# A deadline queue for weight loads, and transposed tiles made in other places

## The chip, the cores and the metric

The kernel runs on one core of one Trainium2 chip. The metric is the device time of one execution in microseconds (us); lower is better. A kernel's time is the median of its runs. The profile's span is about 1.8 us shorter than the time of the same execution (1098.9 us against 1100.72 us for the kernel before), and all times inside a profile count from the start of that span.

## The reference

`x` is 2048 tokens of 1024 values, in bf16. A normalised `x` goes through attention with 32 heads of 32 values, and through a second normalisation and an MLP with 3584 hidden values. The two are multiplied and added to `x`. Cut to what matters:

```python
def _A_ref(x, wqkv, wo):                       # attention, H = 32, Dh = 32
    qkv = (x @ wqkv).reshape(B, S, 3, H, Dh).transpose(2, 0, 3, 1, 4)
    q, k, v = qkv[0], qkv[1], qkv[2]
    p = _softmax(einsum("bhqd,bhkd->bhqk", q, k) * (Dh ** -0.5), axis=-1)
    o = einsum("bhqk,bhkd->bhqd", p, v)
    return o.transpose(0, 2, 1, 3).reshape(B, S, D) @ wo

def _B_ref(x, w1, b1, w2, b2):                 # MLP, F = 3584
    y = _layernorm(x, axis=-1)
    h = _gelu(einsum("bsd,df->bsf", y, w1) + b1)
    return einsum("bsf,fd->bsd", h, w2) + b2

xn = _layernorm(x, axis=-1)
return x + _A_ref(xn, wqkv, wo) * _silu(_B_ref(xn, w1, b1, w2, b2))
```

## The kernel before

The kernel is a host program that writes one instruction list per engine. It walks through 512 units. Each unit has eight score matmuls on PE, two exponentials of 128x1024 on ACT, one filler item on PE (a piece of the MLP, or of the next heads' q, k and v), and the matmuls of the weighted sum (PV). Units 0 to 7 are the prologue: unit p also projects K and Q of the p-th pair of 128-token tiles, then V. For that it needs `xnT`, the normalised `x` with the features on the partitions, one tile after another. Tiles below `TDMA` are transposed on PE and copied by ACT; the others are transposed by DMA. All DMAs are issued by SP, in the order of its list, so a DMA on SP's list waits for everything ahead of it there.

```python
TDMA = 4
def transp(tb):
    i = tb % NXN
    if tb >= TDMA:
        op("sync", lambda e: e.dma_start_transpose(xnT[:, :, tb * 128:(tb + 1) * 128], xnb[i]),
           r=[("xnb", i)], w=[("xnT", tb)], dma=f"xt{tb % 4}", c=256)
        return
    ...                                        # else 8 PE transposes and one ACT copy

def pro_unit(p):                               # units 0 to 7
    if p + 3 < NP:
        norm_pair(p + 3)                       # statistics and normalisation on VectorE; issues transp()
    if p == 3:
        load_bias()
    if p >= 2:
        ynorm_pro(p - 2)                       # the second normalisation of tile p-2, on ACT
    if 4 <= p:
        load_sub(0, p - 4)                     # the first w1 piece (war), a quarter a unit
    pair_kq(p)                                 # 16 matmuls 128x128 by 256
    for t in range(2 * p + 2, 2 * p + 4):
        if t < TDMA:
            transp(t)
    pair_v(p)                                  # 16 more
    ...
def ynorm_pro(tb):
    if tb < 3:
        xt = xst[:, tb * D:(tb + 1) * D]
        op("scalar", lambda e: e.activation(xt, xt, ACT.Identity, ...), ...)
        op("sync", lambda e: e.dma_start(y_d[tb * 128:(tb + 1) * 128, :], xt), ...)   # to a scratch tensor
```

The MLP runs over chunks of 352 tokens. Its input `yTc` (the second normalisation `y`, transposed) is read back from the scratch tensor `y_d` by DMA transposes, at unit 5 for the first chunk. Its weights pass through two buffers (`war`), and the 256 KB pieces of a buffer are put one into each of the following units. The loads of the output stage (`wo`, the residual `xres`, the gate `gres` as a transpose) are spread by unit number as well:

```python
if u == 5:
    for s4 in range(4):
        load_y(0, s4)
...
for v in sorted(k for k in sp_tasks if k <= u):        # sp_tasks[unit] = loads
    for fn, *a in sp_tasks.pop(v):
        fn(*a)
...
if state["qi"] == q_end:                               # the last q, k, v item is done
    tail["xfree"] = pg.lists["tensor"][-1]
    for h in range(HG):
        sp_tasks[u + 1 + 2 * h].append((load_wo, h))
    for t in range(NTB):
        sp_tasks[u + 2 + 4 * t].append((load_xres, t))
...
def pre():                                             # first part of an output item
    if k == 0:
        if tb == 0:
            for t in range(NTB):
                load_gres(t)
```

The host program has a clock model, with a cost for every instruction, only to decide the order in which it writes work into the lists.

The softmax here doesn't subtract the row's maximum and nothing guards it: scores larger than these inputs give would overflow.

## Time and profile before

| | before |
|---|---|
| time, median of 3 runs (lowest to highest) | 1101.85 us (1101.66 to 1102.9) |
| span of the profile | 1098.9 us |
| PE busy, ACT busy | 98%, 95% |
| first scores (unit 0) start at | 17.11 us |
| unit 0 to unit 20 | 61.02 us |
| unit 20 to unit 448 | 876.33 us |
| unit 448 to unit 480 | 64.18 us |
| the rest | 80.26 us |

A stage is read from the timeline as the distance between the first score matmuls of two units.

The page gives the busy time of each engine (part 1: us, share of the span, instructions) and the chain of work that ended last (part 4), for the kernel before:

```profile
PE 1074.6 (98%) x29089; PEld 700.4 (64%) x29089; DVE 629.1 (57%) x1413; ACT 1041.3 (95%) x1190; POOL 20.0 (2%) x63
...
PE 57%; ACT 40%; DVE 1%; DMA 1%; issue 0%; SPq 0%; POOL 0%
```

PE and ACT are both nearly full, and the chain alternates between them. Only what holds up one of these two can cost time. The timeline of PE in the kernel before shows where that is a DMA (columns: start in us, duration in us, engine, line, operation, output and input tiles, shapes, count, and in brackets the idle time before it with its releaser):

```profile
23.52 1.92 PE L675 MATMUL ps<-xnT,wq 128*128 128x256 bf16 x16 [1.53 <-DMA xnT<-hT]
...
46.03 1.92 PE L675 MATMUL ps<-xnT,wq 128*128 128x256 bf16 x16
47.79 1.91 PE L691 MATMUL ps<-wq,xnT 128*128 128x256 bf16 x16
...
54.04 1.11 PE L398 MATMUL ps<-yTc,war 128*32 128x352 bf16 x16 [0.71 <-DMA war<-in_B_w_dram]
...
57.07 0.40 PE L398 MATMUL ps<-wq,xnT 128*32 128x256 bf16 x8 [0.29 <-DMA wq<-in_A_wqkv_dram]
```

The third pair's K and Q projection (23.52) waited 1.53 us for tiles 4 and 5. The first MLP weights came 0.71 us late (54.04). SP's own timeline in the kernel before, where the duration is the time SP takes to issue, shows why:

```profile
18.73 15.05 SPq L382 DMA_TRANSPOSE xnT<-hT  x8
33.83 0.57 SPq L754 DMA_DIRECT2D y_scratch<-OT  x1
35.27 2.60 SPq L382 DMA_TRANSPOSE xnT<-hT  x2
...
38.88 0.37 SPq L754 DMA_DIRECT2D y_scratch<-OT  x1
39.36 2.64 SPq L382 DMA_TRANSPOSE xnT<-hT  x2
...
45.04 5.17 SPq L514 DMA_TRANSPOSE yTc<-y_scratch  x4
50.25 1.09 SPq L493 DMA_DIRECT2D war<-in_B_w_dram  x2
```

A DMA transpose costs SP 1.3 us of issue (2.60 us for two). The four transposes of `y` hold SP from 45.0 to 50.2 us, and the weights that PE wants at 53 us stand behind them.

### The profile page before, as it was taken

How to read it: one execution, taken by the hardware profiler on the slowest of the kernel's cores; microseconds unless marked ns; L12 is line 12 of the kernel's file. 1: busy time of each engine (PE TensorE's matmuls, PEld its weight loads, DVE VectorE, ACT ScalarE, POOL GpSimd, SP SyncE). 2: the span in 40 equal slices, each digit the busy share in tenths (PEclk: the TensorE clock that was granted, in tenths of full speed). 3: DMA queues.
4: the chain of work that ended last, by engine and by line, in shares of the span. 5: the costliest groups of instructions: out<-in, count | busy, mean ns of one | idle time of the engine just before them, and what ended most of it. 6: DMA issues, size and time to landing. Idle time of an engine off the chain costs nothing.

```text
span 1098.9 us, 61692 instructions
## 1 busy us (share of the span) xinstructions
PE 1074.6 (98%) x29089; PEld 700.4 (64%) x29089; DVE 629.1 (57%) x1413; ACT 1041.3 (95%) x1190; POOL 20.0 (2%) x63
## 2 busy tenths in 40 slices
PE   6999999999999999999999999999999999999998
PEld 4766666666666666666666666666666666666665
DVE  8488753377742477652276852277743378624566
ACT  4799999899999999999999999999999999999994
POOL 2400000000000000000000000000000000000000
PEclk9999999999999999999999999999999999999999
DMA  8764256323373224333432334433244324386453
GB/s 249 182 204 138 77 111 175 112 80 109 95 159 96 90 80 128 99 73 105 131 121 80 118 72 133 141 112 109 80 86 136 100 93 147 112 252 115 96 143 99
DMA packets 211624, 132.97 MB, mean 121 GB/s; under 512 B 54698, under 2 KB 202154, under 8 KB 211370
## 3 DMA queue, kind: packets, MB, share of 16 engines
q1 hardware_dynamic: 211370, 129.02, 43.1%
q8 instruction: 228, 3.74, 1.4%
q14 instruction: 26, 0.21, 0.1%
HBM read 104.87 MB, written 12.58 MB: 107 GB/s over the span
## 4 chain that ended last, share of the span: by engine, by line
PE 57%; ACT 40%; DVE 1%; DMA 1%; issue 0%; SPq 0%; POOL 0%
ACT P L836 36%; PE ps L398 34%; PE ps L824 9%; PE ps L853 6%; PE ps L856 6%; ACT u L558 3%; PE ps L675 1%; PE ps L691 1%; DVE stats L326 1%; DMA OT<-in_A_x_dram 1%; ACT thz L601 0%; DMA wq<-in_A_wqkv_dram 0%; DMA xnT<-hT 0%; DVE hT L359 0%; SPq L286 0%
## 5 line engine op out<-in xcount | busy, mean ns | idle before, releaser
L836 ACT ACTIVATE P<-ps 128x1024 bf16<-128x1024 f32 x1024 | 969.7, 1075 | 16.5 <-PE ps L824 10.5
L853 PE MATMUL ps<-P,VP 128*32 128x256 bf16 x4096 | 256.6, 273 | 0.0
L856 PE MATMUL ps<-P,ones 128*32 128x256 bf16 x4096 | 256.5, 273 | 0.0
L398 PE MATMUL ps<-yTc,war 128*32 128x352 bf16 (+1 forms) x5376 | 226.2, 309 | 1.9 <-issue 1.1
L398 PE MATMUL ps<-hT,war 128*32 128x352 bf16 (+1 forms) x5376 | 225.3, 309 | 0.0
L824 PE MATMUL ps<-QT,KT 32*128 32x256 bf16 x4096 | 203.7, 273 | 8.1 <-ACT P L836 5.0
L398 PEld LDWEIGHTS ps<-yTc,war 128*32 128x32 bf16 x5376 | 127.6, 96 | 76.8 <-DVE xb L541 17.3
L398 PEld LDWEIGHTS ps<-hT,war 128*32 128x32 bf16 x5376 | 128.0, 96 | 73.9 <-issue 25.5
L597 DVE TENSOR_SCALAR zh<-ps,b2h 128x352 f32<-128x352 f32 (+1 forms) x48 | 27.5, 573 | 204.4 <-PE ps L398 204.4
L824 PEld LDWEIGHTS ps<-QT,KT 32*128 32x128 bf16 x4096 | 61.0, 92 | 120.6 <-issue 64.2
L541 DVE TENSOR_SCALAR xb<-ps,b1T 128x352 f32<-128x352 f32 (+1 forms) x168 | 96.1, 572 | 63.7 <-PE ps L398 60.0
L853 PEld LDWEIGHTS ps<-P,VP 128*32 128x32 bf16 x4096 | 109.6, 97 | 21.1 <-issue 1.5
L856 PEld LDWEIGHTS ps<-P,ones 128*32 128x32 bf16 x4096 | 109.6, 97 | 18.4
L564 DVE SCALAR_TENSOR_TENSOR hT<-u,xb 128x352 bf16<-128x352 f32 (+1 forms) x168 | 83.8, 508 | 61.3 <-ACT u L558 61.2
L398 PE MATMUL ps<-xnT,wq 128*32 128x352 bf16 (+1 forms) x2688 | 112.7, 309 | 0.0
L398 PEld LDWEIGHTS ps<-xnT,wq 128*32 128x32 bf16 x2688 | 64.0, 96 | 36.8 <-DVE xb L541 10.2
L551 DVE SCALAR_TENSOR_TENSOR u<-u,xb 128x352 f32<-128x352 f32 (+1 forms) x168 | 82.6, 508 | 1.9
L547 DVE TENSOR_TENSOR u<-xb 128x352 f32<-128x352 f32 (+1 forms) x168 | 82.6, 508 | 0.9
L558 ACT ACTIVATE u<-u 128x704 f32<-128x704 f32 (+1 forms) x84 | 70.6, 840 | 0.0
L398 PE MATMUL ps<-xnT,OT 128*32 128x352 bf16 (+1 forms) x1536 | 62.9, 309 | 0.2 <-DVE wq L658 0.2
L398 PE MATMUL ps<-wq,xnT 128*32 128x256 bf16 x1536 | 51.0, 274 | 0.3 <-DMA wq<-in_A_wqkv_dram 0.3
L398 PEld LDWEIGHTS ps<-xnT,OT 128*32 128x32 bf16 x1536 | 37.5, 97 | 19.9 <-DVE wq L658 8.1
(50 smaller groups left out, 468.1 us busy)
## 6 DMA issues: line engine op xcount, KB each, us to landing
war<-in_B_w_dram SPq DMA_DIRECT2D x336, 256.0 KB, 4.1
wq<-in_A_wqkv_dram SPq DMA_DIRECT2D x36, 128.0 KB, 4.2
OT<-in_A_x_dram SPq DMA_DIRECT2D x16, 256.0 KB, 5.6
y_scratch<-OT SPq DMA_DIRECT2D x16, 256.0 KB, 2.5
xnT<-in_A_x_dram SPq DMA_DIRECT2D x16, 256.0 KB, 4.3
out_dram<-wq SPq DMA_DIRECT2D x16, 256.0 KB, 2.0
gT_scratch<-gst SPq DMA_DIRECT2D x40, 88.0 KB, 1.7
xnT<-in_A_wo_dram SPq DMA_DIRECT2D x8, 256.0 KB, 3.6
```

The costliest lines, as they stand in the source:

```text
L326: op("vector", lambda e, c=c: e.bn_stats(stats[:, tb, c, :], xt[:, c * 512:(c + 1) * 512]), r=[("xst", tb)], w=[("st", tb, c)], c=677.0)
L398: ins = e.matmul(outs(j), lhsT=lhs(j), rhs=rhs, start=start, stop=stop, tile_position=(0, 32 * j), skip_group_check=True)
L541: x0 = op("vector", lambda e: e.tensor_scalar(xb[:, 0:n], bank(bk, 0, n), b1T[:, f:f + 1], None, op0=ALU.add), r=[("b", bk), "b1"], w=[kx] ...
L547: x = op("vector", lambda e: e.tensor_tensor(ub[:, 0:n], xb[:, 0:n], xb[:, 0:n], op=ALU.mult), r=[kx], w=[ku], c=151 + 1.042 * n)
L551: x = op("vector", lambda e: e.scalar_tensor_tensor(ub[:, 0:n], ub[:, 0:n], 1.0 / 0.044715, xb[:, 0:n], op0=ALU.add, op1=ALU.mult), r=[kx, ...
L558: x = op("scalar", lambda e: e.activation(ut[:, :, 0:n], ut[:, :, 0:n], ACT.Tanh, scale=0.7978845608028654 * 0.044715), r=kus, w=kus, c=48 ...
L564: op("vector", lambda e: e.scalar_tensor_tensor(hT[:, fq, 0:n], ut[:, i, 0:n], 1.0, xq[:, 0:n], op0=ALU.add, op1=ALU.mult), r=[kus[i], kq] ...
L597: x0 = op("vector", lambda e: e.tensor_scalar(zh[:, 0:n], bank(bk, 0, n), 0.25, b2h[:, nb:nb + 1], op0=ALU.mult, op1=ALU.add), r=[("b", bk ...
L824: ins = e.matmul(bank(bks[j], kh * 256, (kh + 1) * 256), lhsT=KT[i2][32 * j:32 * j + 32, k0:k0 + 128], rhs=QT[i2][32 * j:32 * j + 32, qb * ...
L836: op("scalar", lambda e, p=p, sl=sl: e.activation(pb[:, 2 * p:2 * p + 2, :, :].rearrange("p a b q -> p (a b q)"), ps[:, sl * 1024:(sl + 1) ...
L853: e.matmul(bankq(ACC, j, 0, QW), lhsT=VP[vp][:, kb, vo + 32 * j:vo + 32 * j + 32], rhs=pb[:, j, kh, :], start=first, stop=False, tile_posi ...
L856: ins = e.matmul(bankq(ACC, j, QW, 2 * QW), lhsT=ones[:, 0:32], rhs=pb[:, j, kh, :], start=False, stop=last, tile_position=(0, 32 * j), sk ...
```

## The change

The change wants to take the remaining DMA waits away from PE, and to make the loads follow their deadlines. It has five parts.

1. Tiles 4 and 5 are transposed on PE too (`TDMA` 6).
2. The first chunk's three `y` tiles go by DMA transpose from SBUF straight into `yTc`, and their normalisation moves one unit earlier. They are no longer read back from the scratch tensor (the third, of which the next chunk needs a part, is still stored there as well).
3. The first four weight pieces are loaded at units 2 to 5 in place of 4 to 7.
4. A queue sorted by deadline replaces `sp_tasks`. One load is taken per unit, two if more than three are due, each held until the last PE instruction so far is done (`pace`); in an even unit a normalisation may take their place. A load that is needed and still queued is issued on demand. The output stage's loads are in the queue, the first four `gres` transposes too.
5. The clock model's constants change.

The diff, cut to its core:

```diff
-        TDMA = 4
+        TDMA = 6
@@ prologue
-            if p >= 2:
-                ynorm_pro(p - 2)
-            if 4 <= p:
-                load_sub(0, p - 4)
+            if p >= 1:
+                ynorm_pro(p - 1)
+            if 2 <= p < 2 + 4:
+                load_sub(0, p - 2)
@@ ynorm_pro
-                op("sync", lambda e: e.dma_start(y_d[tb * 128:(tb + 1) * 128, :], xt), ...)
+                m = min(128, CW - tb * 128)
+                op("sync", lambda e: e.dma_start_transpose(yTc[:, :, tb * 128:tb * 128 + m], xt[0:m, :]), ...)
+                if m < 128:
+                    op("sync", lambda e: e.dma_start(y_d[tb * 128:(tb + 1) * 128, :], xt), ...)
-            if u == 5:
-                for s4 in range(4):
-                    load_y(0, s4)
@@ the queue
+        def soon(prio, tag, fn, *a):
+            due.append((prio, len(due), tag, fn, a))
+            due.sort(key=lambda z: z[0])
+        def run_due(tag=None):
+            i = 0 if tag is None else next((i for i, z in enumerate(due) if z[2] == tag), None)
+            ...
+            fn(*a)
-                for v in sorted(k for k in sp_tasks if k <= u):
-                    for fn, *a in sp_tasks.pop(v):
-                        fn(*a)
+                if u % 2 == 0 and ys and not any(z[0] < cnt["piece"] + 2 for z in due):
+                    ynorm(ys.pop(0))
+                else:
+                    pace[:] = pg.lists["tensor"][-1:]
+                    for _ in range(1 + (len(due) > 3)):
+                        run_due()
+                    pace.clear()
@@ output stage
                     for h in range(HG):
-                        sp_tasks[u + 1 + 2 * h].append((load_wo, h))
+                        soon(NPC + 2 * h, ("wo", h), load_wo, h)
                     for t in range(NTB):
-                        sp_tasks[u + 2 + 4 * t].append((load_xres, t))
+                        soon(NPC + 16, ("xres", t), load_xres, t)
+                        soon(NPC + 16, ("gres", t), load_gres, t)
@@ clock model
-            self.dma_clk = max(t, self.dma_clk) + 4.4 * c
+            self.dma_clk = max(t, self.dma_clk) + 3.4 * c
-                t = max(t, self.clk[eng] + 103.0)
-                span += max(120.0 - one, 0.0)
+                t = max(t, self.clk[eng] + (98.0 if mode == "col" else 105.0))
+                span += 11.0
[... cut: wq and w1/w2 pieces put into the queue with soon(), on-demand calls of run_due() in the items ...]
```

## The prediction

> **What bounds the kernel now.** The page gives PE 98% and ACT 95% of a 1098.9 us span; the chain that ended last is PE 57%, ACT 40%, DMA 1%. From 57 us on the loop alternates between a full PE and a full ACT: a unit with a w1 item repeats every 2.07 us on PE (timeline, 57.84, 59.91, 61.98), two exponentials every 1.83 us on ACT. The windows view has PE idle for 7.3 of the 880 us from 120 to 1000 us. The waits view shows no PE wait on a DMA after 57.3 us. The long waits are SP's own (380 us before war loads) and cost nothing.
>
> **What is exposed** lies before 60 us. In timeline and waits, PE waits 7.5 us for the first normalised tile (untouched), 1.53 us at 23.5 us for the DMA transpose of tiles 4 and 5 (issued at 18.7), 0.45 us for ACT at 52.2, 0.71 us for war at 54.0, 0.29 us for wq at 57.1. On SP the four y transposes take 45.0 to 50.2 us; two war and four wq loads queue behind them.
>
> **Costs and gains.**
> 1. Tiles 4 and 5 on PE: removes the 1.53 us wait; adds 1.2 to 1.4 us of PE (16 transposes took 1.37 us at 14.06) and 1.9 us of ACT (two evictions, 1.94 us at 15.02). The first y normalisation (about 1.15 us of ACT) moves from the time of that wait into the same crowded unit. My sum puts the third pair's KQ matmuls at 24.1 us instead of 23.5: zero or a loss of up to 0.7 us. Later pairs keep their 4.48 us period, bound by PE.
> 2. y straight from SBUF: removes the scratch round trip of chunk 0 and 5.2 us of SP at 45 to 50 us. With war loaded two units earlier the 0.71 us wait goes.
> 3. wq for the second V pair starts before 51.4 us, but pacing holds its last parts until the next unit's scores, so the 0.29 us wait may stay or grow to 1 us. Net of 2 and 3: 1 to 2 us gained.
> 4. Paced loads in the loop: about one load a unit; 256 KB landed in 4.1 us (DMA issues), two units. I expect no new waits.
> 5. Altered cost constants move each unit of the host's schedule model by under 10 ns. They may reorder VectorE tasks and tanh; either sign, 2 to 3 us. Evictions already hold weight loads for some 65 us in total (waits of PEld).
> 6. Tail: gres loads go earlier, but PE never waited for them.
>
> The Trainium skill ("DMA: Bandwidth & Descriptors", "Issuing engines are not separate DMA queues") says all issuers share 16 DMA engines; that agrees with a gain from order, not bandwidth (mean DMA share 43%).
>
> **Predicted:** 1098.5 us, about 0.3% faster; range 1094 to 1102.5. Faster by over 2%: 0.02; within 2%: 0.95; slower by over 2%: 0.03.
>
> **Right or wrong.** Right: no DMA wait on xnT near 23 us, KQ of the third pair at 23.5 to 24.3 us; no y transposes at 45 to 50 us; no war wait at 54 us; the tenth unit's scores at 56 to 57.5 us instead of 57.84; the later span within 3 us of before. Wrong: PE waits on war or wq in the loop (a load popped only on demand costs about 4 us), or a third pair later than 25 us.
>
> **What would make it wrong.** The queue serving weights late at the changes between w1, w2 and wq; or new constants improving the interleaving of ACT and PE by more than I allow, where up to 10 us lie.

## The result, and the profile after

The changed kernel is correct. It ran at 1103.52 us (1102.71 to 1104.61, 4 runs) against 1102.38 us for the kernel before (1101.66 to 1102.97, 4 runs) in the same rounds: a ratio of 1.0011, with an interval of 0.9994 to 1.0029. A ratio here and below is the mean time of one kernel's fast runs over that of the other's of the same rounds, so it is not quite the ratio of the quoted medians. The change is worth nothing measurable, and the prediction of 1098.5 us (1094 to 1102.5) missed.

For scale: the 32 runs of the kernel before that were made beside the experiments lie between 1099.8 and 1105.5 us. One trace of each is therefore not enough, and both kernels were traced twice more (experiments e13 to e16). The stages in all six traces, in us:

| trace | first scores | unit 0 to 20 | of it unit 6 to 7 | of it unit 7 to 10 | 20 to 448 | 448 to 480 | span |
|---|---|---|---|---|---|---|---|
| before | 17.11 | 61.02 | 4.48 | 8.20 | 876.33 | 64.18 | 1098.9 |
| before, e13 | 17.28 | 62.51 | 4.48 | 10.24 | 876.16 | 64.28 | 1100.5 |
| before, e15 | 16.85 | 62.52 | 4.48 | 8.22 | 876.00 | 65.67 | 1101.3 |
| after | 17.70 | 63.16 | 8.22 | 6.55 | 875.53 | 65.85 | 1102.5 |
| after, e14 | 17.43 | 63.58 | 8.18 | 6.55 | 875.85 | 68.28 | 1105.4 |
| after, e16 | 17.06 | 62.32 | 6.09 | 6.95 | 875.51 | 66.42 | 1101.7 |

The rest, from unit 480 to the end, takes 80.3 to 80.4 us in every trace. Between the means of the three traces, the change costs 1.0 us up to unit 20, gains 0.5 us in the loop and costs 2.1 us from unit 448 to 480. The first traces alone give 3.6 us of longer span: 0.59 at the first scores, 2.14 up to unit 20, minus 0.80 in the loop, and 1.67 from 448 to 480. The start of the first scores (16.5 to 18.1 us over all traces) follows the moment when the PE clock comes up (13.4 to 16.6 us in the clock record) and not the change.

The same two parts of the page, for the kernel after:

```profile
PE 1077.6 (98%) x29105; PEld 701.4 (64%) x29105; DVE 630.4 (57%) x1413; ACT 1043.0 (95%) x1192; POOL 20.0 (2%) x63
...
PE 54%; ACT 44%; DVE 1%; DMA 1%; SPq 0%; issue 0%
```

PE has 16 instructions and 3.0 us more to do: the 16 transposes, and matmuls that ran slower for a while. PE's timeline in the kernel after:

```profile
21.96 1.92 PE L699 MATMUL ps<-wq,xnT 128*128 128x256 bf16 x16 [1.11 <-ACT QT L689]
...
24.70 1.92 PE L683 MATMUL ps<-xnT,wq 128*128 128x256 bf16 x16
...
49.28 3.00 PE L683 MATMUL ps<-xnT,wq 128*128 128x256 bf16 x16 [2.00 <-DMA xnT<-hT]
52.08 2.54 PE L699 MATMUL ps<-wq,xnT 128*128 128x256 bf16 x16
54.55 0.40 PE L836 MATMUL ps<-QT,KT 32*128 32x256 bf16 x8
```

The wait of 1.53 us for tiles 4 and 5 is gone. In its place PE waits 1.11 us for ACT at 21.96, and the third pair starts at 24.70 us. The waits for `war` and `wq` are gone too: unit 7 to unit 10 takes 6.55 us in place of 8.20. But the eighth pair now waits 2.00 us for its DMA transposes, and then its 16 matmuls take 3.00 and 2.54 us where they took 1.92 and 1.91. SP's timeline in the kernel after:

```profile
36.42 2.59 SPq L379 DMA_TRANSPOSE xnT<-hT  x2
39.06 0.60 SPq L310 DMA_DIRECT2D brow<-in_B_b_dram  x1
39.72 0.27 SPq L311 DMA_DIRECT2D brow<-in_B_b_dram  x1
40.03 1.22 SPq L763 DMA_TRANSPOSE yTc<-OT  x1
41.30 0.59 SPq L766 DMA_DIRECT2D y_scratch<-OT  x1
41.92 0.44 SPq L503 DMA_DIRECT2D war<-in_B_w_dram  x1
42.46 4.28 SPq L379 DMA_TRANSPOSE xnT<-hT  x2
```

Each entry starts within 0.1 us of the end of the one before: SP is the resource that is full here. The `y` transposes and the first weight loads now stand ahead of tiles 14 and 15, which are issued at 42.46 us where they were issued at 39.36 us, and take 4.28 us to issue in place of 2.64. The windows view of the kernel after (window, length, busy us and instruction count of PE, PEld, DVE, ACT and POOL, then the granted clock, the DMA share and GB/s) shows the rest:

```profile
45.00:50.00 5.00, 3.00 (x44) 2.11 (x43) 0.00 (x0) 2.78 (x5) 3.93 (x15) 0.99 0.93 210
50.00:55.00 5.00, 5.00 (x41) 3.42 (x42) 0.00 (x0) 1.00 (x3) 0.00 (x0) 0.66 0.03 9
```

After the wait the granted clock is 0.66 over the next 5 us. The clock record holds it at one half for 3413 ns and at full speed otherwise; 3.413 us at a half in 5 us make 0.66. The DMA engines are nearly idle by then (0.03), so the slow matmuls are a matter of the clock.

Late in the kernel, the timeline of PE shows holes in the middle of a unit that wait for no semaphore, as here in the kernel after:

```profile
975.49 0.28 PE L865 MATMUL ps<-P,VP 128*32 128x256 bf16 x4
975.60 0.28 PE L868 MATMUL ps<-P,ones 128*32 128x256 bf16 x4
976.63 0.29 PE L865 MATMUL ps<-P,VP 128*32 128x256 bf16 x4 [0.75 <-issue]
```

The windows view there, of the kernel before:

```profile
975.00:980.00 5.00, 4.95 (x156) 3.59 (x151) 0.97 (x2) 5.00 (x8) 0.00 (x0) 1.00 0.95 289
980.00:985.00 5.00, 5.00 (x164) 3.72 (x156) 0.98 (x2) 4.53 (x6) 0.00 (x0) 1.00 0.67 199
985.00:990.00 5.00, 5.00 (x158) 3.44 (x152) 1.19 (x3) 4.91 (x7) 0.00 (x0) 1.00 0.60 173
```

and of the kernel after:

```profile
975.00:980.00 5.00, 4.25 (x132) 2.92 (x124) 1.23 (x4) 4.58 (x6) 0.00 (x0) 1.00 0.97 290
980.00:985.00 5.00, 5.00 (x160) 3.48 (x154) 0.97 (x2) 4.71 (x7) 0.00 (x0) 1.00 1.10 249
985.00:990.00 5.00, 4.41 (x140) 2.96 (x132) 0.98 (x2) 3.84 (x5) 0.00 (x0) 1.00 0.84 245
```

PE falls from full to 4.25 and 4.41 us of 5, while the DMA share stays about 1 for ten microseconds longer. The queue has bunched the output stage's loads together with the last weight pieces: in SP's timeline five `wo` loads go out in a row at 962.00 us, where the kernel before sends them one at a time, the last at 980.02 us.

### The profile page after: what moved, and what is told of

It reads as the page before. It is cut to its first block, busy times and chain, and to the rows that moved or that the text cites. A ratio compares the mean times of both kernels' runs of the same rounds, so it can differ in the third digit from the quotient of the medians.

```text
span 1102.5 us, 61718 instructions
## 1 busy us (share of the span) xinstructions
PE 1077.6 (98%) x29105; PEld 701.4 (64%) x29105; DVE 630.4 (57%) x1413; ACT 1043.0 (95%) x1192; POOL 20.0 (2%) x63
## 3 DMA queue, kind: packets, MB, share of 16 engines
q8 instruction: 228, 3.74, 1.5%
## 4 chain that ended last, share of the span: by engine, by line
PE 54%; ACT 44%; DVE 1%; DMA 1%; SPq 0%; issue 0%
ACT P L848 39%; PE ps L395 32%; PE ps L836 9%; PE ps L865 5%; PE ps L868 5%; ACT u L565 4%; PE ps L683 1%; PE ps L699 1%; DMA xnT<-hT 0%; ACT thz L609 0%; SPq L379 0%; DMA OT<-in_A_x_dram 0%; PE ps L386 0%; DVE stats L323 0%; ACT xnT L389 0%
```

## The experiments

Two theories came out of the traces. **Theory A**: the new `y` transposes and early weight loads fill SP, so that tiles 14 and 15 are issued late, and the wait that follows also brings a stretch of half clock. **Theory E**: in the tail, the doubled rate of the queue and the early `gres` transposes fill the DMA engines, and PE then runs dry because its instructions are fetched late. Their rivals were: **B**, the bytes of the weight loads and not SP's order delay the transposes; **C**, the queue or the constants make the whole loop slower (the table above refutes it: unit 20 to 448 takes 875.5 to 875.9 us after and 876.0 to 876.3 before); **D**, the third pair's later start (part 1) delays everything after it; **F**, the pacing or the clock constants cause the loss in the tail.

In all of them "before" is the kernel before in the same rounds. All kernels gave correct results. Each run also reports its mean granted clock: 0.998 or less in every traced run with a stretch of half clock after the start, and 0.999 or 1.0 in every traced run without.

### e1: the weight loads back at units 4 to 7

```diff
-            if 2 <= p < 2 + 4:
-                load_sub(0, p - 2)
+            if 4 <= p:
+                load_sub(0, p - 4)
```

> Edit to the changed kernel: only the four war loads of the prologue go back to units 4 to 7, as before the change; the y transposes stay early. Theory A (SP order): the last two xnT transposes (tiles 14, 15) were issued at 42.46 us and landed near 49 us because SP, which spends about 1.3 us on each transpose, had y work and war loads of units 2 and 3 in front of them. Two war loads (0.57 and 0.44 us) then account for about 1 us of the 3 us delay: issue of tile 14 near 41.3 us, the wait of the eighth pair's KQ falls from 2.0 us to under 1 us, and the half-clock window after it (3.4 us, worth 1.7 us) goes[...]. Rival B (the 16 DMA engines are full, the war bytes of 0.5 MB slow the transposes): the wait goes altogether, because the war bytes were what held the transposes. Rival C (the paced queue or the constants make the loop slower): no change of the total. A: 2 to 3.5 us faster than the changed kernel's slower runs (span near 1099.5 to 1100.5).

Measured: 1102.87 us against 1103.24 us, ratio 0.9999 (0.9982 to 1.0016). The wait of the eighth pair fell from 2.00 to 0.57 us; tile 14 was issued at 41.99 us. Unit 6 to 7 took 5.12 us, with no half clock in it. The weight loads ahead of the transposes are part of the cause, and not all of it. They do not act by their place on SP alone: tile 14 was expected at 41.3 us, and measured from the first scores (which began 0.28 us earlier here) it was issued only 0.2 us sooner than in the kernel after. More came from the issue of the two transposes, which took 3.56 us in place of 4.28. The median is 0.65 us below the changed kernel's, where 2 to 3.5 us were expected.

### e2: the third `y` tile's transpose behind tiles 14 and 15

```diff
+            if p == 4:
+                yturn_pro(2)          # the DMA transpose and the store of y tile 2, no longer in ynorm_pro
```

> Edit to the changed kernel: only the transpose of y tile 2 and its store to scratch are put behind the transposes of tiles 14 and 15; war loads stay early. Theory A: takes 1.2 + 0.6 us of SP away from in front of them; tile 14 issued near 40.5 us, the wait of the eighth pair's KQ under 0.7 us, no half-clock window, span 1099 to 1100. Rival B (war bytes on full DMA engines): the wait stays near 2 us, since the early war loads stay. Rival C: no change of the total.

Measured: 1102.47 us against 1103.24 us, ratio 0.9999 (0.9982 to 1.0016). SP's timeline in e2:

```profile
39.87 0.40 SPq L503 DMA_DIRECT2D war<-in_B_w_dram  x1
40.37 2.59 SPq L379 DMA_TRANSPOSE xnT<-hT  x2
```

Tile 14 was issued at 40.37 us, PE did not wait for `xnT` at all, and unit 6 to 7 took 4.53 us. All weight loads stayed where the change had put them, so their bytes alone are not the cause: in that form rival B is refuted. What counts is what stands ahead on SP. (The `y` tile's SP time and its bytes moved together, so the run does not separate these two.) The long issue of tiles 14 and 15 also goes with the `y` tile's transpose and store directly ahead of it: it took 4.28 us in the kernel after, 3.56 in e1 and 4.31 in e4, where they stand there, and 2.59 us in e2 and e3, where they do not. The DMA share does not explain it (0.78 during the 4.28 us, and 0.78 during the 2.64 us of the kernel before); the reason stays open.

### e3: both

```diff
[the edits of e1 and e2]
```

> Edit to the changed kernel: both of the above. Theory A: tile 14 issued as soon as VectorE has normalised it (39.3 us), no wait of the eighth pair's KQ, no half-clock window; its loop starts (scores of the eighth unit) near 50.8 us instead of 54.55, scores of the eleventh unit near 57.4 us against 57.84 of the kernel before and 61.10 of the changed one; span 1098.5 to 1099, time about 0.3 to 0.5 us below the kernel before, 3.5 us below the changed kernel's slower runs. Rival C: the loop part after the eleventh unit is longer than before's 1041.1 us and the total stays at 1102 or more.

Measured: 1101.42 us against 1103.24 us, ratio 0.9992 (0.9977 to 1.0008). Timelines of e3, SP first, then PE:

```profile
39.55 2.59 SPq L379 DMA_TRANSPOSE xnT<-hT  x2
42.20 1.97 SPq L770 DMA_TRANSPOSE yTc<-OT  x1
...
46.62 1.92 PE L683 MATMUL ps<-xnT,wq 128*128 128x256 bf16 x16
...
50.22 0.40 PE L843 MATMUL ps<-QT,KT 32*128 32x256 bf16 x8
```

Tile 14 is issued at 39.55 us, nearly where the kernel before had it. The eighth pair waits for nothing, runs at full clock, and the scores of unit 7 start at 50.22 us in place of 54.55. Unit 0 to 20 takes 59.47 us, 3.7 us less than in the changed kernel's first trace and 1.6 us less than in the best trace of the kernel before. Theory A holds, and the gain that was predicted for parts 2 and 3 is there. The median shows little of it (0.3 to 0.5% was expected), because the tail still loses (unit 448 to 480: 66.37 us).

### e4: `TDMA` back to 4

```diff
-        TDMA = 6
+        TDMA = 4
```

> Edit to the changed kernel: tiles 4 and 5 go back to DMA transposes, all else kept. Theory A: the transposes of tiles 14 and 15 are late as before (SP is busy without a break from tile 8 on, and tiles 4 and 5 come well ahead of that), so the 2.0 us wait and the half-clock window stay; the third pair's KQ waits for the DMA again, about 1.5 us, and starts near 23.5 to 24 us: span within 1 us of the changed kernel's 1102.5. Rival D (transposing tiles 4 and 5 on PE is what cost): span falls to 1099 or less.

Measured: 1103.87 us against 1103.24 us, ratio 1.0016 (0.9997 to 1.0036). The third pair started at 23.60 us again, but the eighth pair waited 2.34 us and a half clock followed. PE also waited 1.27 us for the bias load (`brow`), which SP issued at 39.27 us, behind two `y` transposes and a weight load; the changed kernel shows this wait in e14 and e16 too (0.4 and 0.8 us), the kernel before in none of its traces. Rival D is refuted: the eighth pair's wait does not come from the third pair. Nor does part 1 make it shorter: measured from the first scores, tile 14 was issued after 24.55 us here and after 24.76 us in the kernel after.

### e5: e3, and the first four `gres` transposes back at the first output item

```diff
 [the edits of e3]
                 if k == 0:
+                    if tb == 0:
+                        for t in range(NTB):
+                            load_gres(t)
...
-                        soon(NPC + 16, ("gres", t), load_gres, t)
```

> Edit to the run with y tile 2 and war late: the gres transposes of the first four output tiles go out when the first output item begins, as before the change, instead of from the queue right after the last war piece. In all five traces of the changed family PE lost 1.7 to 3.5 us between units 457 and 464 (about 972 to 990 us) against the kernel before; the gaps lie in the middle of matmul groups that wait for no semaphore, each ends with an instruction fetch of 16 KB on queue 8, and the DMA share there is 1.0 to 1.2 against 0.6 to 0.95 before. Theory E (the queue bunches loads at the end: gres transposes and xres beside the last war pieces fill the 16 DMA engines, PE's instruction fetch comes late): the gaps between 975 and 990 us go, DMA share there under 1.0; a gap near 972 us may stay; the loss between units 457 and 464 falls from about 2.2 us to under 1 us; span 1097 to 1098.3. Rival F (PACE waits or the constants cause it): the loss stays at about 2.2 us.

Measured: 1100.34 us against 1102.01 us, ratio 0.9978 (0.9963 to 0.9993). Unit 448 to 480 took 65.54 us where e3 took 66.37. That is the direction of theory E, but the step is smaller than the spread of the changed kernel's own traces (65.85 to 68.28 us). The expectation was met in part: between units 457 and 464, where the loss sits, the run took 16.13 us against 14.78 in the kernel before, so 1.35 us remained where under 1 us was expected. PE still had one issue gap of 0.7 us.

### e6: e3, and the second load per unit only when weight pieces are due

```diff
 [the edits of e3]
-                    for _ in range(1 + (len(due) > 3)):
+                    for _ in range(1 + (sum(z[0] < NPC for z in due) > 3)):
```

> Edit to the run with y tile 2 and war late: loads of the tail (wo, xres, gres) no longer count towards popping two loads in a unit; only war, wq and y do. gres stays in the queue. If the doubled rate of the tail loads is what starves the instruction fetch (theory E, burst of wo), the gap near 972 us goes and those at 975 to 990 us shrink: loss under 1 us. If the gres transposes are the ones that matter, gaps at 980 to 990 us stay or move later: loss 1 to 2.5 us.

Measured: 1102.59 us against 1102.01 us, ratio 0.9999 (0.9978 to 1.0021). The windows view of e6, to be held against that of the kernel after above:

```profile
975.00:980.00 5.00, 4.97 (x160) 3.66 (x156) 0.97 (x2) 4.97 (x7) 0.00 (x0) 1.00 0.59 174
980.00:985.00 5.00, 5.00 (x167) 3.68 (x156) 0.98 (x2) 4.51 (x6) 0.00 (x0) 1.00 0.70 188
```

At a DMA share of 0.59 and 0.70 PE is full and there is no issue gap, and units 457 to 464 took 14.78 us, as in the kernel before. The `gres` transposes, though still in the queue, went out late as well (the first at 997.04 us, against 977.78 us in the kernel after), so this run removed the doubled rate and the early `gres` together. But the `wo` loads are now late for the output items: PE stood idle for 2.04 us before the item at 1000.97 us, with a half clock after it, and unit 448 to 480 took 68.07 us. The waits view books this wait on VectorE, whose semaphore came last; the loads of `wo` in front of it tell the rest. The gap that was to be removed is gone, and another has replaced it.

### e7: the queue and the constants alone

```diff
[TDMA, ynorm_pro, the y transposes and the first weight loads as in the kernel before]
```

> The kernel before with the queue, the pacing and the cost constants alone: y of the first chunk through scratch as before, tiles 4 to 15 by DMA, prologue order as before. Theory (A plus E): prologue as before (third pair's KQ near 23.5 us after a DMA wait of about 1.5 us, no wait of the eighth pair, scores of the eleventh unit at 57.3 to 58.5 us), loop as before up to unit 450, then the same loss of 1.5 to 3.5 us at 972 to 990 us with unexplained PE gaps: span 1100 to 1102. Rival C (the loop is slower throughout): the difference grows steadily from unit 60 on.

Measured: 1102.23 us against 1102.01 us, ratio 0.9994 (0.9975 to 1.0012). The prologue is that of the kernel before (unit 6 to 7: 4.48 us), and unit 448 to 480 took 65.54 us, with issue gaps of 0.6 and 0.3 us. The 65.54 us lie within what the kernel before shows in its three traces. Units 457 to 464 do not: they took 15.62 us, against 14.57 to 14.80. So the loss at the eighth pair belongs to parts 2 and 3, and a loss in the tail comes with parts 4 and 5, here 0.8 us and less than the 1.5 us expected.

### e8: a first try at a better version

```diff
[TDMA 5; ynorm_pro(p - 2) at p >= 2; load_bias at p == 0; all four weight loads at p == 4;
 the gres edit of e5 and the queue edit of e6]
```

> A version meant to beat both: changed kernel with tile 4 turned on PE and tile 5 by DMA; y normalisation one unit later (out of the crowded second unit); bias loads in unit 0; war loads together in unit 4 behind tiles 14 and 15; gres late; tail loads counted singly. Expected: third pair's KQ at 22.6 to 23.6 us, no DMA wait of the eighth pair, scores of the eleventh unit at 55.3 to 56.6 us (before 57.84), no issue gaps at 972 to 990 us: span 1096 to 1097.5, time about 0.3% below the kernel before. If it is not below before, a cost that I have not named sits in the loop.

Measured: 1105.75 us against 1102.01 us, ratio 1.0026 (1.0011 to 1.0041). This is the slowest version of the change. Its prologue is the fastest so far (unit 0 to 20: 58.55 us), but the `wo` loads were late as in e6: PE waited 1.47 and 4.37 us, all six runs had a stretch of half clock, and unit 448 to 480 took 71.79 us. It shows how little it takes to lose in the tail what the prologue gained.

### e9: e3, with the output stage's loads set by unit number again

```diff
 [the edits of e3]
+                for v in sorted(k for k in sp_tail if k <= u):
+                    for fn, *a in sp_tail.pop(v):
+                        fn(*a)
...
-                        soon(NPC + 2 * h, ("wo", h), load_wo, h)
+                        sp_tail[u + 1 + 2 * h].append((load_wo, h))
-                        soon(NPC + 16, ("xres", t), load_xres, t)
-                        soon(NPC + 16, ("gres", t), load_gres, t)
+                        sp_tail[u + 2 + 4 * t].append((load_xres, t))      # gres at the first output item
-                    for _ in range(1 + (len(due) > 3)):
+                    for _ in range(1 + (len(due) > (7 if tail else 3))):
```

> The changed kernel with two repairs only: y tile 2 and the war loads behind tiles 14 and 15 (as in the third experiment), and the loads of the output stage (wo, xres, first four gres) issued by unit number as in the kernel before, not by the queue; after the last Q and K item the queue pops one load a unit unless more than seven are due. Theory A plus E: no DMA wait of the eighth pair, scores of the eleventh unit near 57.0 us, 1.2 to 1.5 us ahead of before at unit 20 once the start of the first unit is taken off, and no loss over 0.5 us between units 448 and 480: span 1096.3 to 1098, time 0.15 to 0.25% below before. If a loss of 1.3 us or more stays at 972 to 990 us, the queue's tail loads were not its cause.

Measured: 1099.69 us (1098.6 to 1100.15) against 1102.4 us, ratio 0.9972 (0.9958 to 0.9987). The time is clearly below both kernels. The trace, however, lost 1.40 us in the tail (65.58 us), where under half a microsecond was expected. The kernel before lost as much in one of its own three traces (e15, 65.67 us), so that size varies from run to run, and one trace does not settle it. Between units 457 and 464 it lost 0.96 us (15.74 us), less than the 1.3 us that the expectation had named as its refutation, but not nothing.

### e10: the best version

```diff
[the edits of e9 in the tail, and in the prologue: TDMA 5; ynorm_pro(p - 2) at p >= 2;
 load_bias at p == 0; y tile 2 as in the change; and]
-            if 2 <= p < 2 + 4:
-                load_sub(0, p - 2)
+            if p == 4:
+                for q in range(4):
+                    load_sub(0, q)            # behind the transposes of tiles 14 and 15
```

> The eighth experiment (which lost 7.6 us to wo loads that came too late, and was 2.6 us ahead of before until then) with the output-stage loads by unit number as in the kernel before. Expected: same prologue (scores of the eleventh unit 0.9 to 1.9 us ahead of before), no wait for wo near 998 us, no loss at 972 to 990 us: span 1095.5 to 1097, time 0.25 to 0.4% below before.

Measured: 1098.07 us (1097.21 to 1098.91) against 1102.4 us, ratio 0.9962 (0.9949 to 0.9974). It beats both kernels. Unit 0 to 20 took 58.54 us, unit 448 to 480 took 64.43 us (units 457 to 464: 14.82 us), and none of its five runs had a stretch of half clock. Its windows view in the tail:

```profile
975.00:980.00 5.00, 5.00 (x156) 3.51 (x152) 0.98 (x2) 4.53 (x7) 0.00 (x0) 1.00 0.84 252
980.00:985.00 5.00, 5.00 (x164) 3.71 (x160) 0.46 (x1) 4.79 (x6) 0.00 (x0) 1.00 0.43 126
```

### e11: the changed kernel with 16 dummy matmuls in front of the eighth pair

```diff
+                if p == 7 and off == 0:
+                    # 16 matmuls on tiles 0 and 1, which are there; the result is overwritten
+                    op("tensor", g, r=[("wq", 1, s) for s in range(4)] + [("xnT", 0), ("xnT", 1)], w=[("b", bk)], ...)
```

> The changed kernel with 16 extra full-width matmuls (results overwritten) put on PE just before the eighth pair's KQ, where it waits 2.0 us for tiles 14 and 15; they need about 1.75 us. It tells the wait itself from the slow clock after it. If the 1.7 us lost behind the wait are due to the clock that is granted at half for 3.4 us after an idle PE: the records show no half-clock stretch near 50 us, KQ and V of the eighth pair take 1.92 us each again (3.00 and 2.54 in the changed kernel's trace), the scores of the eighth unit come 5.3 to 5.8 us after the first matmul of that KQ's ready time, that is near 52.5 us rather than 54.55, span about 1100.8, although PE has 1.75 us of useless work more. If the slowness comes from DMA traffic or memory contention, KQ and V stay at 3.00 and 2.54 us and nothing is gained.

Measured: 1103.22 us against 1102.4 us, ratio 1.0008 (0.9992 to 1.0023). PE's timeline in e11:

```profile
47.55 1.92 PE L689 MATMUL ps<-xnT,wq 128*128 128x256 bf16 x16
49.32 1.92 PE L683 MATMUL ps<-xnT,wq 128*128 128x256 bf16 x16
51.08 1.91 PE L706 MATMUL ps<-wq,xnT 128*128 128x256 bf16 x16
52.92 0.40 PE L843 MATMUL ps<-QT,KT 32*128 32x256 bf16 x8
```

The first line is the dummies, in the place of the wait. The pair starts as late as before (49.32 us against 49.28), but now runs at 1.92 and 1.91 us, and unit 6 to 7 takes 6.25 us in place of 8.22. So the idle time in front is what brings the half clock, and the half clock alone costs about 2.0 us here. The other part of the loss, the late start, remains. None of the four runs had a half clock; as the changed kernel had it in only one of its four, the count by itself would not show this.

The clock record shows which idle time it is. In each trace the half clock starts a whole number of windows of 3.413 us after the clock came up (10 in the kernel after, 12 in e13, 3 in e15). The windows view gives PE's busy time in the last window before it: 1.41 us in the kernel after, 1.61 in e14, 1.52 in e13, 1.56 in e15 and 1.14 in e12. In e16 the wait of 1.5 us fell across two windows, with 2.39 and 2.90 us busy, and no half clock followed. Up to the end of the work, in all 18 traces, no window in which PE was busy for more than half was followed by a half clock; of those with less, one was not (1.57 us, from 984.5 us in e14), so the pattern has an exception.

### e12: the kernel before, with its tail loads bunched

```diff
 (on the kernel before)
-                        sp_tasks[u + 1 + 2 * h].append((load_wo, h))
+                        sp_tasks[u + 1 + h].append((load_wo, h))
-                        sp_tasks[u + 2 + 4 * t].append((load_xres, t))
+                        sp_tasks[u + 9 + t].append((load_xres, t))
+                        sp_tasks[u + 9 + t].append((load_gres, t))     # no longer at the first output item
```

> The kernel before with nothing of the change, but its output-stage loads bunched: wo one a unit instead of one in two, then xres and gres of the first four tiles one a unit, beside the war loads of one a unit. Theory E (bunched loads fill the DMA engines and delay PE's instruction fetch): DMA share 0.95 to 1.2 from 965 to 985 us (0.85 to 0.95 before), PE gaps of 0.5 to 1.5 us inside matmul groups that wait for no semaphore, a loss of 0.8 to 3 us between units 450 and 470, nothing before. Rival F (the pacing waits on PE, or the constants, make the loss): no loss, since neither is in this kernel.

Measured: 1107.08 us (1106.39 to 1107.4) against 1102.4 us, ratio 1.0042 (1.0028 to 1.0056). The waits of PE from 950 to 1018 us in e12 (engine, line, releaser, then us in total, how often, the longest):

```profile
PE ps L398 <- DMA war<-in_B_w_dram: 1.9, 1, 1.9
PE ps L398 <- issue: 0.7, 1, 0.7
...
PE ps L821 <- issue: 0.4, 1, 0.4
```

This kernel has no queue, no pacing and the old constants. Unit 448 to 480 took 67.95 us, 3.8 us more than in the first trace of the kernel before; 1.9 us of it is a true wait for a weight piece and 1.1 us are issue gaps. The DMA share was 1.17 and 1.19 from 975 to 985 us. Bunched loads are enough to cause the gaps: rival F is not needed, and e10, which keeps the pacing and the constants, has no loss there.

### e13 to e16: both kernels again, unchanged, in turn

> The kernel before, unedited, for a second trace. Theory E (the queue's bunched tail loads delay PE's instruction fetch) needs that the kernel before loses nothing there: units 448 to 480 take within 0.6 us of the 64.18 us of its first trace. If they take 65.5 us or more, the first trace was lucky and the loss is chance, not the queue. Prologue: the wait for war near 54 us lies between 0.7 us (first trace) and 2.3 us (the same prologue in the twelfth experiment), with a half-clock stretch behind it when it is over 2 us.

> The changed kernel, unedited, for a second trace. Theory A: the eighth pair's KQ waits 1.5 to 2.5 us for tiles 14 and 15 again, since SP's order is fixed; the half-clock stretch may or may not follow. Theory E: units 448 to 480 take 65.5 to 67.8 us (first trace 65.84) against 64.18 before.

> The kernel before, unedited, for a third trace: units 448 to 480 within 0.6 us of 64.18 us if theory E holds.

> The changed kernel, unedited, for a third trace: the eighth pair's KQ waits 1.5 to 2.5 us; units 448 to 480 take 65.5 to 67.8 us if theory E holds.

Measured, single runs on one chip: before 1102.38 and 1103.1 us, after 1107.2 and 1103.5 us (a further run of the kernel before, shared by all four: 1103.38 us). The stages stand in the table above. Two things follow.

First, the wait of the eighth pair is in all three traces of the changed kernel (2.0, 2.2 and 1.5 us) and in none of the kernel before. The half clock after it is in two of three: it did not follow the wait of 1.5 us (in that trace PE had also waited 0.8 us for the bias load before it). The kernel before has a stretch of half clock as well in two of its three traces, elsewhere: after the wait of 1.76 us for `war` in e13 (the expectation had named over 2 us), and after a wait of 1.8 us for `xnT` in e15. Its first trace, on which the prediction was built, had neither and was its shortest.

Second, the tail. By the measure, unit 448 to 480, theory E failed once: the kernel before took 65.67 us in e15, where 0.6 us around 64.18 was the limit, and the changed kernel took 68.28 us in e14, over the 67.8 named. So chance has a share in the size of this loss. The narrower stretch named in e5, units 457 to 464, keeps the two apart: 14.78, 14.80 and 14.57 us before, 16.44, 18.01 and 16.28 us after. The issue waits of PE from 950 to 1018 us in the waits view are none in the kernel before and in e13, and 1.4 us in e15. In the changed kernel they are 0.7, 3.4 and 1.2 us. The longest, in e14, in the waits view:

```profile
PE ps L865 <- issue: 2.2, 1, 2.2
```

What PE waits for there is shown by the DMA view of the first trace of the changed kernel, from 974 to 978 us, around the gap of 0.75 us (queue and kind, packets, MB, share of 16 engines):

```profile
q1 hardware_dynamic: 1599, 1.13, 95.1%
q8 instruction: 1, 0.02, 1.4%
```

A single packet of the instruction queue, of 16 KB, falls among 1599 packets of loads. Such a packet comes every 4.6 us anyway, so this alone proves little, but the packed traces say more. In the kernel after, queue 8 carried 228 packets and PE had 58378 instructions: one packet for 256 of them. From 960 to 999 us, 13 of the 18 traces have 29 gaps of PE over 0.3 us, besides the wait for `war` in e12. Every one of them ends at the same place in a block of 256 instructions (at matmul 16 to 18 of 128, counted from the kernel's first), and 1.24 to 1.64 us after a packet of queue 8 has landed; the wait for `war` ends at matmul 97. So what PE lacks in these gaps is its next block of instructions, also where the waits view books one on ACT (0.59 us before 986.00 us in the kernel after). Why the block comes late is argued and not shown: the DMA share in the 4 us before each gap was 0.71 to 1.41, and the gaps went where the loads were spread (e6, e10). No run shortened the instruction list or moved a fetch, so the fetch itself was not varied.

### What stays open

How much of the tail's loss is due to the doubled rate and how much to the early `gres` transposes is not settled: e5 (only `gres` moved) reached a ratio of 0.9978 and e9 (both undone) 0.9972, with overlapping intervals, and no run moved the rate alone. Why e9 still lost 0.96 us with the loads spread, and why e15 had gaps of 1.0 and 0.4 us with nothing changed, is open. The constants alone, and `TDMA` 6 alone on the kernel before, were not run. The length of a wait does not tell whether a half clock follows: 1.76 us (e13) was followed by one, 1.93 us (the wait for `war` in e12's tail, at a clock of 1.00 in the windows view) was not. There PE was busy for 1.87 of the 3.41 us of that window, more than half; e11 gives the pattern and its one exception.

## Why the prediction was wrong

The prediction is held here against the sum that it was built of, and the kernels against each other in runs of equal clock. The runs whose reported clock was 1.0 have these mean spans: before 1100.4 us (16 of 32 runs beside the experiments), after 1101.5 us (3 of its 4 runs), e3 1100.0 us (5 runs), e9 1097.7 us (5 runs), e10 1096.3 us (5 runs). These are from several chips, so they serve to order the kernels, not to give a last digit. They also show that the half clock does not explain the equal medians: the kernel before has it in 15 of its 32 runs, the changed kernel in 1 of its 4. By difference they put 1.5 us on the eighth pair (after to e3), and 2.3 us on the tail (e3 to e9); the traces of e3 and e9 show only 0.8 us of the latter between units 448 and 480, so the 2.3 us lean on runs without a trace.

- **Step 1, third pair: right.** Predicted was KQ at 24.1 us, and zero to 0.7 us lost. In e3, whose first scores start at the same 17.11 us as in the kernel before, it began at 24.10 us against 23.52 there (24.70 us in the changed kernel's first trace, whose scores began 0.59 us later). The wait for `xnT` near 23 us went away as said; the moved normalisation on ACT took most of it back (PE waits 1.11 us for ACT).
- **Step 1, "Later pairs keep their 4.48 us period, bound by PE": this step failed.** The pair from unit 6 to 7 took 8.22, 8.18 and 6.09 us. The prediction counted what the `y` transposes freed on SP at 45 to 50 us, and did not add up what they put on SP before 43 us. By the after timeline that is 2.17, 1.30 and 1.22 us for three transposes, 0.59 us for the store and 1.01 us for two weight loads: 6.3 us of issue, against 0.94 us for two stores in the kernel before. SP has no room left for it, because every transpose of `xnT` costs it 1.3 us too. The two transposes also took 1.64 us longer to issue. e2 and e3 take the wait away by moving entries of SP's list. A half clock, which the prediction did not consider, added about 2.0 us in two of three traces (e11). So the marker that the prediction had set itself was missed: the tenth unit's scores, counted from 0, began at 61.10 us and not at 56 to 57.5; in e3 they began at 56.81 us.
- **Steps 2 and 3, 1 to 2 us: right in size.** Unit 7 to 10 went from 8.20 to 6.55 us, a gain of 1.65 us; in e3 it is 6.59 us. It was spent before it could be seen, by the wait one unit earlier.
- **Step 4, "I expect no new waits": right in the loop, wrong in the tail.** From unit 20 to 448 the changed kernel is 0.5 us faster in the mean of three traces, with no PE wait on `war`. From 448 to 480 it is 2.1 us slower, and the new stops of PE there are for instructions, which the step did not consider.
- **Step 5: right that it was small.** It cannot be told apart from the queue in the loop.
- **Step 6, "gres loads go earlier, but PE never waited for them": this reading failed as an argument.** PE still never waits for `gres`. But loads that nobody waits for cross the DMA engines together with the last weight pieces and with the instruction packets (95.1% and 1.4% of the 16 engines in the DMA view above), and PE stops there for 0.3 to 2.2 us at a time. The bunched loads are shown as the cause from both sides: units 457 to 464 took 14.78 us in e6 and 14.82 in e10, where they are spread, and 18.54 us in e12, where the kernel before got them bunched. e9, with 0.96 us left, is the exception.
- **The number itself.** The steps that had a size summed to about 1.2 us gained, the middle of 0 to 0.7 lost and of 1 to 2 gained. The predicted 1098.5 us is 3.35 us below the time before. About two microseconds of it had no step with a size under them; step 5 left the interleaving open by 2 to 3 us either way, and the whole loop gave 0.5 us.

The prediction quoted the Trainium skill, "DMA: Bandwidth & Descriptors", section "Issuing engines are not separate DMA queues": all issuers share the same 16 DMA engines. No run here tests that, since SP issues every DMA of these kernels. The same section says that the issue time is usually small relative to the DMA itself. For the transposes of this kernel that is not so: 1.3 us of issue each against 4.0 us from issue to landing, on one engine that issues all of them, and that made SP the limit of the prologue.

## What to carry to other kernels

When work is moved earlier, add it to the issuing engine's own line at the new place and ask which later deadline stands behind it there; a DMA that takes 1.3 us to issue uses up an engine that looks idle on the page. A load that no engine waits for can still cost time if it is sent in a bunch, so spread prefetches up to the moment they are needed, and check that they are not late either (e6 and e8). Build a forecast from several traces: the one used here was 1.6 to 2.4 us shorter than the two others of the same kernel.

## What the Trainium skill lacked or had wrong

- "DMA: Bandwidth & Descriptors", "Issuing engines are not separate DMA queues", says that the time to initiate a DMA is usually small relative to the DMA. For a DMA transpose of a 128x1024 bf16 tile, SP was held 1.3 us (2.59 us for two), and once 4.28 us for two, at a DMA share of 0.78; the section "DMA Transpose (X-bar)" of the same page gives no issue time.
- "TensorE: Matmul & The Clock Gate", "What's actually happening", says that the clock falls to a half after at least one idle window, and that a window is 3413 ns. The length agrees: each stretch at a half lasted 3413 ns in these traces. But waits well under a window were followed by such a stretch (2.00 us in the kernel after, 1.76 us in e13, 2.34 us in e4), and others were not (1.5 us in e16, 1.93 us in e12), so no rule by length alone fits these runs. Nor had the window to be idle: PE was busy for up to 1.61 us of the 3.41 us window before a half clock (e14), and below half in each such window.
- "Runtime: NRT & Kernel Launch", "Terms", says that instruction memory is refilled in 16 KiB blocks, which agrees with the packets of 16384 bytes seen here; its preamble note says that the fetch has its own port. No page says that a kernel's own loads may delay it. Here PE stopped at the end of a block of 256 instructions for 0.3 to 2.2 us, waiting for no semaphore, where the DMA share was 0.71 to 1.41.
- "CRC Debugging", "Comparing the Two Runs", puts the instruction refills on queue 14. In the trace of the kernel before, queue 8 carried 228 instruction packets with 3.74 MB, and queue 14 carried 26 with 0.21 MB.
